# One written order for another: where each part of a fused attention and gated-MLP kernel stands, with the same parts and buffers

## The chip, the core and the metric

The kernel runs on one core of a Trainium2 chip. The metric is the device time of one execution in microseconds (us), lower is better. The engines that matter are TensorE (PE in the profile), VectorE (DVE), ScalarE (ACT), GpSimd (POOL) and SyncE (SP), which issues nearly all loads and stores.

## The reference

Windowed attention (8 batches, 8 heads, 576 positions, head size 64, window 64), its output laid out as 4608 tokens of 512 features, an RMS norm, and a gated MLP (512 to 1536 to 512):

```python
scores = scale * np.matmul(q, k.transpose(0, 1, 3, 2))
scores = np.where((rel >= 0) & (rel < window), scores, -1000000000.0)   # rel = query position - key position
attn = np.exp(scores - np.max(scores, axis=-1, keepdims=True))
attn = attn / (np.sum(attn, axis=-1, keepdims=True) + 1e-09)
x = np.matmul(attn, v)                      # (B, H, S, D), then transposed to (4608, 512)
rms = np.sqrt(np.mean(x * x, axis=-1, keepdims=True) + 1e-06)
xn = x / rms * rms_g
g = xn @ w_gate
silu = g * (1.0 / (1.0 + np.exp(-g)))
return silu * (xn @ w_val) @ w_out
```

## The kernel before

**Tiles.** The 64 heads are 32 pairs, four to a batch. The 4608 tokens are 9 tiles of 512. The 1536 inner features are worked on in chunks. A float32 operand of the MLP is split into a high and a low half-precision part, and a product is then three matmuls (high by high, high by low, low by high), `three` at L1391 to L1393. Tiles 0 and 1 are multiplied so, in groups of 12 matmuls into one PSUM bank. Tiles 2 to 8 use a seven-product scheme (L1694, 12 matmuls each) and outer products (L1633). The weights prepared for these lie in DRAM (`sevens`, `outer`) and are loaded again for every chunk (L1604, L1614), 512 or 768 KB at a time.

**Parts.** The program consists of 3,894 named parts. In the opening (batches 0 and 1 and the first token tiles) the names are a letter and indices: for head pair n, `s` scores on PE, `m` masks on DVE (L735, each followed by an accumulator read), `a` exponential on ACT, `i` sum and reciprocal on DVE (L818, L819), `w` scaling on POOL (L825, L827), `t` transposes on PE (L833), `u` copies, `v` values on PE, `y` take. For the weights: `d` load, `e` exponent on ACT, `p` product on PE (L522), `r` rest on DVE (L526), `t` reduction on DVE (L563, with other indices), `h` and `l` the high and low halves (`l00` and `l01` on DVE, L554). For the normed tokens of tile 0: `F` scaling on DVE (L1299), `H` the high part (L1302, on DVE or ACT by piece), `L` the low part (L1307, on POOL for this tile); `F00x` are a piece of 512 tokens, `F01x` one of 64. `G0cim` is a gate (m = 0) or value (m = 1) group of tile 0, `A M N O P` what follows it. Loads are `q`, `k`, `j`, `d`, `g`. Later parts have numbers: a leading dot is an attention pair (`.10` the scores of a pair, `.10.22` the turn of its mask, DVE L711, after a way through DRAM, L701 and L707; `.11` its values, PE L897; `.65` and `.217` loads of keys and values, `.66` and `.218` the scores that use them), and `+u602` is a product of chunk 6, `+u602.0` the load that follows it into the buffer that it freed; `+o…` are the outer products and `+g…` gate groups of tile 1.

**Order.** `SEQUENCE` (L44 on) writes all parts in one total order. The program emits them in that order, and each engine's queue is then fixed by it:

```python
AT = {n: k for k, n in enumerate(SEQUENCE.split())}
...
for ins in traced[start:]:
    if ins.engine in before and ins.engine in WRITTEN(nc):
        tc.add_manual_dep(ins, before[ins.engine].name, ..., reason="written order")
```

So an instruction waits for the one written ahead of it on its own engine, and for the data and buffers that it needs. `HOMES` gives for each ring of SBUF buffers which buffer the k-th tile takes. A PSUM bank is the one that has been free longest:

```python
def any_bank(name):
    bank_of[name] = free_banks.pop(0)
def done_with(name):
    free_banks.append(bank_of.pop(name))
```

so the order also decides which bank a group gets, and whose last reader it waits for. In this order `G0000`, the first gate group, takes the bank that held half of the scores of pair 5 (`s50`), and the first three masks of `m500` are its last readers. The scores' bank is given back by the mask that reads it last, the bank of the norm's broadcast (`rb`) by the last scaling, `F003`.

Of the kernel before, what the change touches and what calls it, by code (L numbers as in the profile page):

```python
# [52 lines left out]
w411 q7 N000 i50 t411 w501 k6 L010 t410 O000 P000 m511 d30 e301 L013 z11 z12 h10 e300 p210 r210 s60 t20 p211 r211 m600 m601 d40 v40 y40 h11 G0011 t21
z20 p301 d31 u410 u411 p300 t501 y0 l10 a600 a511 z21 A001 z22 l11 z13 a601 z14 w500 t500 u500 M001 v41 G0100 G0110 G0101 y41 N001 x21 h21 a510 e310
e311 r300 i51 s61 r301 t30 u501 A011 M011 v50 i60 h20 m610 m611 l21 w510 t510 u510 p311 r311 O001 w600 P001 p310 a610 A010 w511 G0111 t511 l20 G0200
r310 t31 y50 z30 M010 d41 e411 N011 z31 z32 x30 w601 t601 N010 e410 p410 e400 p411 G0201 r411 r410 q4q a611 i61 w611 w610 t600 z23 u511 u600 e401 O010
v51 y51 k7 s71 u601 q5q P010 z33 j6 .231 s70 m700 a700 v60 m701 p400 r400 a701 h30 l30 m710 A020 i70 m711 t610 .229 G0210 u610 a711 p401 r401 t40 t611
u611 t41 .8 .230 G0211 z40 w701 .0 w700 y60 t700 v61 M020 N020 d50 a710 i71 w711 G0300 d51 e510 e511 p511 A021 t701 x31 M021 N021 w710 p510 h31 z41
z42 h40 A030 j7 r510 e500 G0310 t710 u700 u701 .228 .228.3 l31 y61 x41 r511 d62 u710 O011 O021 P021 t711 G0311 v70 e501 l40 p500 q6q d60 p501 G0301
d63 r500 u711 v71 r501 M030 y70 O020 P020 e621 e620 p621 A031 r621 p620 r620 G0400 b5 d61 e600 P011 M031 N031 .1 e601 h41 t50 t51 O031 e630 z50 p600  # L60
r600 y71 q7q f62 G0410 z43 A041 N030 O030 l41 z51 z52 h50 .230.2 p601 r601 x51 h51 b6 z24 G0401 l50 b7 R1 S1 e631 G0411 p630 r630 p631 r631 B10 F100
A040 F101 F102 F103 .9 P031 M040 N040 f60 O040 B11 l51 H101 H102 G0500 z53 G0511 A050 H103 H100 F110 M041 N041 L100 e610 d65 G0510 e611 A051 p611 L101
F111 p610 .26 L103 G0501 P030 d64 e640 O041 L102 M051 N051 M050 f63 O051 P041 G1000 .234 F112 r611 z34 N050 r610 e641 p640 p641 r640 r641 A100 e650
f61 .2 .2.0 .2.6 .2.5 .2.14 f64 M100 .10 .10.0 .10.5 .10.1 G1011 .10.6 e651 O050 p650 .2.3 .228.1 .228.4 F113 .228.5 .2.7 .233 P051 .10.3 .10.12 H22
p651 .228.6 P040 .2.8 .10.14 r650 r651 f65 G1001 N100 .228.7 .228.8 O100 .17 P100 o0 .228.10 .2.1 G1010 .228.9 .228.11 H11 .228.0 o1 o2 h61 D3 .229.3
.10.7 G1100 G1101 h60 .229.1 .229.4 A110 .2.12 .2.17 .10.8 .10.17 .18 l60 h62 l62 H21 G1110 h64 .10.2 .2.16 .10.4 .10.13 .229.5 .10.11 .2.2 .229.6
.229.7 .229.8 .234.0 .230.0 l61 .2.4 h63 G1111 U10 U30 M110 l64 l63 L11 A111 M111 N111 .229.10 .229.9 .229.11 .10.9 Ht3 A101 Lt3 M101 .236 h65 l65
.231.0 .2.13 .19 N101 .10.10 O101 .19.1 .19.3 .2.10 .235 P101 .19.12 D1 Ht1 U20 .19.0 .19.2 .19.4 .19.11 P050 .2.9 U11 .231.3 U00 Lt1 U21 .2.15 .2.11
# [1940 lines left out]
```

## Time and profile before

| | us |
|---|---|
| median of 3 executions | 934.73 (934.68 to 938.94) |
| the profiled execution | 933.47 |
| its span (first to last instruction) | 931.7 |
| around the span | 1.77 |
| PE busy | 904.0 |
| PE idle | 27.7 |

The span is the stretch that the trace covers; the 1.77 us around it are not in the trace. Times in the rows below are counted from the start of the span. A matmul's length in the trace overlaps that of the next one, so the pace is read from the starts.

### The profile page before, as it was taken

To read this page: it belongs to the slowest core of one execution; us is meant where nothing else is said; L and a number is where in the kernel's file an instruction comes from. 1 tells how busy PE (TensorE), PEld (TensorE's weight loads), DVE (VectorE), ACT (ScalarE), POOL (GpSimd) and SP (SyncE) were. 2 spreads that over 40 slices of the span, in tenths; PEclk is the share of its full clock that TensorE was granted. 3 is DMA by queue.
4 is the path that set the end of the run, shared out by engine and by line. 5 is a ranking of instruction groups with operands and counts; after the bars stand their busy time and mean duration, and the time that the engine had idled before them with its cause. 6 is when DMAs were issued, how large, how long until landed. Compare 5 with 4: busy or idle time off the path is not lost.

```text
span 931.7 us, 22882 instructions
## 1 busy us (share of the span) xinstructions
PE 904.0 (97%) x8581; PEld 688.2 (74%) x8581; DVE 704.1 (76%) x1919; ACT 567.8 (61%) x1473; POOL 413.3 (44%) x486
## 2 busy tenths in 40 slices
PE   5889999999999999999999999999989999999998
PEld 4645554444447885688888888888878888888887
DVE  6899788967797789789767888887777787734760
ACT  5977886744446655667666666776647556524551
POOL 3342562335336353554462666453514645420440
PEclk8889999999999999999999999999999999999999
DMA  8655471368676975787668858975876557546551
GB/s 294 206 177 198 147 256 39 99 184 232 200 225 194 295 279 164 248 299 239 255 203 293 295 177 287 308 245 179 278 268 225 177 163 256 186 138 226 188 159 46
DMA packets 105438, 198.62 MB, mean 213 GB/s; under 512 B 27760, under 2 KB 64624, under 8 KB 105328
## 3 DMA queue, kind: packets, MB, share of 16 engines
q1 hardware_dynamic: 104752, 195.99, 64.9%
q8 instruction: 67, 1.10, 0.5%
q10 hardware_dynamic: 576, 1.18, 0.4%
q14 instruction: 43, 0.35, 0.1%
HBM read 159.39 MB, written 37.75 MB: 212 GB/s over the span
## 4 chain that ended last, share of the span: by engine, by line
PE 74%; DVE 8%; DMA 7%; issue 4%; POOL 3%; ACT 3%; SPq 1%; DVEq 0%; POOLq 0%; ACTq 0%
PE a L1694 31%; PE o L1633 16%; PE po L1391 3%; PE po L1392 3%; PE po L1393 3%; PE sc L722 3%; PE x L897 2%; DMA wt<-sevens 2%; DMA pm<-via 2%; PE pg L1391 2%; PE pg L1392 2%; PE pg L1393 2%; PE pv L1391 2%; PE pv L1392 1%; PE pv L1393 1%
## 5 line engine op out<-in xcount | busy, mean ns | idle before, releaser
L1694 PEld LDWEIGHTS <-wt 128*128 128x128 f16 x3528 | 342.8, 98 | 48.4 <-DMA wt<-sevens 3.4
L1694 PE MATMUL a<-xn,wt 128*128 128x256 f16 x2016 | 237.5, 273 | 1.1 <-DMA wt<-sevens 0.9
L1694 PE MATMUL a<-wt,wt 128*128 128x256 f16 x1224 | 148.1, 273 | 2.0 <-DMA wt<-sevens 1.6
L1731 ACT ACTIVATE th<-a,hsc 128x256 f32<-128x256 f32 x168 | 78.6, 473 | 103.0 <-DVE a L1795 70.1
L1766 POOL TENSOR_TENSOR h<-th,h 128x512 f16<-128x512 f32 x84 | 98.3, 1176 | 81.8 <-ACT h L1764 80.9
L1766 POOL TENSOR_TENSOR wt<-u,wt 128x512 f16<-128x512 f32 (+1 forms) x72 | 67.5, 939 | 134.8 <-ACT wt L1764 88.2
L1633 PE MATMUL o<-wt,h 128*128 128x256 f16 x864 | 100.3, 273 | 0.2 <-DVE o L1655 0.2
L1795 DVE TENSOR_TENSOR a<-a,s 128x512 f32<-128x512 f32 x90 | 62.1, 693 | 48.8 <-PE a L1694 43.8
L1633 PEld LDWEIGHTS <-h 128*128 128x128 f16 x864 | 84.0, 98 | 11.4 <-issue 1.4
L1726 DVE SCALAR_TENSOR_TENSOR th<-th,a 128x256 f32<-128x256 f32 x168 | 69.2, 412 | 29.0 <-ACT th L1731 27.6
L738 ACT ACTIVATE pm<-pm,st 128x128 f32<-128x128 f32 (+1 forms) x216 | 83.8, 390 | 11.0 <-DVE st L735 10.8
L693 POOL TENSOR_TENSOR pm<-pm,st 128x512 f32<-128x512 f32 (+1 forms) x72 | 60.2, 864 | 46.7 <-DVE st L767 25.6
L1727 DVE SCALAR_TENSOR_TENSOR th<-a,th 128x256 f32<-128x256 f32 x168 | 71.3, 424 | 5.8
L1633 PEld LDWEIGHTS <-wt 128*128 128x128 f16 x648 | 63.3, 98 | 8.5 <-issue 1.2
L1712 ACT COPY s<-a 128x512 f32<-128x512 f32 x90 | 52.2, 582 | 22.0 <-PE a L1694 19.2
L1764 ACT CAST h<-th 128x512 f16<-128x512 f32 x84 | 51.2, 615 | 13.5 <-DVE th L1742 7.9
L735 DVE CUSTOM_DVE_ANT_0 pm<-sc,blocked 128x128 f32<-128x128 f32 x192 | 48.9, 281 | 12.5 <-PE sc L722 12.3
L1391 PE MATMUL po<-wt,h 128*128 128x512 f16 x136 | 51.6, 379 | 0.0
L1392 PE MATMUL po<-wt,h 128*128 128x512 f16 x136 | 51.5, 379 | 0.0
L1393 PE MATMUL po<-wt,h 128*128 128x512 f16 x136 | 51.5, 379 | 0.0
L722 PE MATMUL sc<-kv,q 64*64 64x128 f32 (+1 forms) x1056 | 43.5, 291 | 5.9 <-DMA q<-q 4.9
L1633 PE MATMUL o<-wt,wt 128*128 128x256 f16 x432 | 49.1, 273 | 0.0
(235 smaller groups left out, 1757.0 us busy)
## 6 DMA issues: line engine op xcount, KB each, us to landing
wt<-sevens SPq DMA_DIRECT2D x84, 512.0 KB, 5.1
wt<-sevens SPq DMA_DIRECT2D x42, 768.0 KB, 5.7
wt<-outer SPq DMA_DIRECT2D x24, 768.0 KB, 5.7
kv<-kv SPq DMA_DIRECT2D x28, 608.0 KB, 5.7
via<-pm SPq DMA_DIRECT2D x96, 144.0 KB, 2.7
pm<-via SPq DMA_DIRECT2D x24, 576.0 KB, 4.7
q<-q SPq DMA_DIRECT2D x28, 288.0 KB, 4.7
st<-w_gate SPq DMA_DIRECT2D x6, 1024.0 KB, 6.8
```

Source lines behind the costliest of these rows:

```text
L722: nc.tensor.matmul(out.rearrange("p (n c) -> p n c", c=D), lhsT=qt[hd, j * D : (j + 1) * D], rhs=halves[hd, :1, :] if j == 0 else halves[h ...
L738: nc.scalar.activation(part, part, AF.Exp, bias=low, scale=-1.0, accum_out=total)
L1391: nc.tensor.matmul(acc, lhsT=lh, rhs=rh, start=first, stop=False)
L1392: nc.tensor.matmul(acc, lhsT=lh, rhs=rl, start=False, stop=False)
L1393: nc.tensor.matmul(acc, lhsT=ll, rhs=rh, start=False, stop=last)
L1633: nc.tensor.matmul(acc[:, sub * HT : (sub + 1) * HT], lhsT=l[:, x, sub * P : (sub + 1) * P], rhs=r[:, y, :], start=first and c == cs[0] an ...
L1694: nc.tensor.matmul(acc[:, i * HT : (i + 1) * HT], lhsT=ws[l][:, kt, :], rhs=b[:, m, kt, :], start=at_start, stop=kt == 1 and j == 2, skip_ ...
L1726: nc.vector.scalar_tensor_tensor(cols, cols, 1.0, acc[:, :HT], ALU.add, ALU.mult)
L1727: nc.vector.scalar_tensor_tensor(cols, acc[:, HT:], 2.0**-42, cols, ALU.mult, ALU.mult)
L1731: nc.scalar.activation(cols, acc[:, :HT], AF.Tanh, scale=th_scale[:, c : c + 1])
L1766: nc.gpsimd.tensor_tensor(lo, src, hi, ALU.subtract)
L1795: nc.vector.tensor_tensor(to, acc, kept.pop((c, name)), ALU.add)
```

## The change

One part of the file is replaced: the text of `SEQUENCE`, and with it `HOMES`. The same 3,894 names stand in another order; no part, no shape, no engine of an instruction and no number of buffers is changed. With the order change which buffer of its ring a tile takes (`HOMES` is the list for the new order), which PSUM bank a group takes, and when each load is issued. The diff, cut to the stretches that the prediction speaks of:

```diff
@@ -42,190 +42,190 @@
 SEQUENCE = """
-q0 k0 s00 q1 q2 m000 a000 m001 a001 i00 k1 s10 s01 m010 j1 c10 m100 w001 a010 a100 k2 s21 m011 a011 j0 g0 m101 a101 g1 j2 s11 w000 t000 t001 c21 g2
...
-b3a y31 q3q b3 R0a e200 S0a R0 S0 z01 z02 z03 B00a B00 F001 F002 H002 F000 F003 L002 e100 e101 p100 s41 p101 a400 d11 e110 r101 B01 F010 r100 e201 k5
-p201 j5 q5 s50 H003 F012 H001 e111 p110 a401 F011 i40 L001 r110 H000 L000 w400 m410 h01 s51 m411 d21 H010 F013 h00 l00 p111 m500 a500 m501 p200 r111
-w401 a411 t401 L003 G0000 l01 H012 L012 r200 t400 t10 a501 t11 r201 e210 A000 z10 a410 i41 G0001 H011 L011 u400 u401 H013 w410 M000 e211 m510 G0010
...
-.10.22 .37 +g1200.0 +g1200.1 +g1201 +g1201.0 .11 +g1201.0.0 .12 +g1310 +g1310.0 .234.2 .19.21 .238 .13 .19.22 .20 .21 .234.1 .234.4 .234.5 E0 .234.6
...
-+u602 +u605.0 .189.15 .188.21 +u606 .188.22 +u602.0 +u602.1 .189.16 .189.17 +u602.2 +o542 +u606.0 .189.18 .200.18 .189.19 .200.19 +u602.2.0 .189.20
-+u603 +o542.0 +o542.1 +o542.2 .192.22 +o542.2.0 .189.21 +u611 +u603.0 +u612 +u603.1 +u603.2 +u603.2.0 +u607 +u611.0 +u616 +u607.0 +u604 +u604.0
-+u612.1 +u612.2 +u612.2.0 .209 .209.0 +u607.1 +u607.1.0 +u604.1 .209.2 .209.11 .209.5 .216 .200.20 .193 .194 .209.6 +u615 .195 .196 +u615.0 +u607.2
-+u607.4 +u604.1.0 .209.1 +u607.5 +u621 +u621.0 +u622 +u607.3 .209.7 +u616.0 +u607.6 .209.8 +u612.0 +u613 .209.3 +u613.1 +u613.2 .209.4 .209.10 .227
-.209.16 +u607.7 +u604.2 +u604.4 +u613.2.0 +u617 +u617.0 +u617.1 .217 +u622.1 +u626 +u626.0 +u617.1.0 +u617.2 +u607.8 +u632 +u625 +u625.0 +u631 +u614
-+u622.2 .200.21 +u617.4 .200.22 +u622.2.0 +u613.0 +u631.0 +u632.1 .218 .218.2 .218.1 .209.15 +u614.1 .218.7 .209.14 .218.0 .218.5 .209.9 +u622.0
...
+q0 k0 s01 m010 q2 j0 c01 s00 m000 m001 k1 q1 s10 m011 a010 m100 a000 a001 i00 a011 i01 g0 g1 g2 a100 m101 c00 a101 i10 d00 e001 e000 w000 t000 u000 k2
...
+q3a b3a y31 z01 z02 R0a q3q b3 S0a R0 S0 e110 e111 p110 p111 e101 B00a r111 B00 q5 F000 d20 h00 k5 s50 F002 F001 e200 H000 L000 r110 H002 L002 e201
+p201 p200 q7 e100 p101 p100 l00 q6 a411 H001 L001 F003 m500 r201 a500 H003 L003 z03 r100 h01 B01 G0000 r101 l01 G0001 a401 a400 k6 r200 i40 w400 t400
+t10 t11 m501 d21 e210 e211 a410 p210 z10 u400 j5 i41 r210 p211 F010 F011 A000 M000 r211 j4 d30 G0011 z11 a501 w411 e300 w401 F012 w410 F013 t401 z12
...
+.233.7 .233.8 .233.10 +g1401 +g1201.0 .28.10 .28.12 .10.22 .233.9 .233.11 +g1201.0.0 +g1210.0 +g1210.1 .36 +g1211.0 .28.9 .28.16 .28.18 .28.19 .28.20
+.235.1 +g1300 +g1300.0 +g1500 +g1500.0 +g1300.1 +g1301.0 +g1301.0.0 +g1201.0.1 .251 +g1501 .19.22 .234.1 +g1500.1 +g1501.0 .11 .13 .20 .12 .234.3
...
+.209.11 .192.19 +u602.1 +u602.2 +u606 .200.16 +o572.0 +u606.0 +o542 +o542.0 .189.8 +u611 +u602.2.0 .209.7 .189.21 .189.5 .209.10 +o572.2.0 +u611.0
+.189.22 .216 .192.20 .209.13 .189.6 +u603 +o542.2 +u603.1 .200.9 .200.14 .200.15 .200.12 .200.18 +u616 +u603.2 +u603.2.0 +u602.0 +u607 +u607.0 .192.21
+.189.10 +u612 +u612.1 +u607.1 +u607.1.0 +u615 +u607.2 +u607.4 .209.0 +u615.0 .209.8 +u612.2 +u607.5 +u604 +u613 +o542.1 +u621 .192.22 .193 .209.9
++u607.3 +u604.1 +u616.0 +u607.6 +u613.1 +u613.2 .200.19 .200.20 .194 .209.15 .195 +u613.2.0 +u604.1.0 .189.14 .196 +u607.7 +u604.2 +u621.0 +u617
++u617.0 +u604.4 +u604.6 .209.17 +u622 +u622.1 .209.12 +u625 +u625.0 +u614 +u617.1 .209.16 +u603.0 +u626 +u626.0 +o542.2.0 +u612.2.0 +u617.1.0 +u617.2
++u617.4 +u604.0 +u622.2 .217 .218 .218.1 .218.6 .218.5 .197 .218.7 +u614.1 +u604.3 .209.18 .209.19 +u612.0 +u622.0 .189.18 +u623 +u607.8 .218.3
++u617.5 +u617.7 +u623.1 +u623.2 +u614.0 +u622.2.0 .218.12 +u627 +u623.2.0 +u627.0 +u627.1 +u617.3 .218.15 +u627.1.0 +u604.5 +u631 +u631.0 .218.10
++u613.0 +u635 +u624 +u624.1 .200.21 +u632 .218.14 +u614.1.0 +u617.6 .200.22 .218.0 +u635.0 +u627.2 .218.16 +u627.3 +u623.0 +u614.3 .189.19 .218.8
...
```

In words: `F003` stands later among DVE's parts and is now what frees `G0000`'s bank; `G0000` and `G0001` come ahead of other parts of the opening; `.11` stands two groups further behind `.10.22`; the loads `+o542.0`, `+u602.0` and `+u612.0` change places.

## Rows read from the trace of the kernel before

**Rows 1.** Page, part 1: busy us (share of the span) and instructions of each engine.
```profile
PE 904.0 (97%) x8581; PEld 688.2 (74%) x8581; DVE 704.1 (76%) x1919; ACT 567.8 (61%) x1473; POOL 413.3 (44%) x486
```

**Rows 2.** Windows of the span: length, busy us (x instructions) by engine, PEclk, DMA share, GB/s.
```profile
6.37:54.68 48.31, 37.08 (x425) 26.14 (x426) 41.30 (x197) 38.60 (x120) 20.36 (x32) 0.82 0.70 243
54.68:58.90 4.22, 4.22 (x12) 1.65 (x13) 4.19 (x11) 3.60 (x15) 0.84 (x1) 0.60 0.52 165
58.90:97.00 38.10, 37.43 (x321) 20.38 (x319) 33.87 (x101) 28.41 (x68) 15.56 (x25) 1.00 0.57 193
```

**Rows 3.** Waits of PE, 0 to 195 us: total us, times, longest us.
```profile
PE pg L1391 <- DVE st L735: 2.2, 2, 2.0
```

**Rows 4.** Waits of PE, 195 us to the end.
```profile
PE a L1694 <- DMA wt<-sevens: 2.5, 3, 1.6
PE x L897 <- DVE pm L711: 1.7, 2, 1.2
PE s L722 <- ACT pm L738: 1.1, 1, 1.1
PE a L1694 <- DVE xb L979: 0.4, 1, 0.4
```

**Rows 5.** Timeline of PE around the first gate group: start, length, instruction, [idle before <-releaser].
```profile
50.84 0.66 PE L722 MATMUL sc<-kv,q 64*64 64x128 f32 x14 [0.93 <-DVE wt L526]
...
52.30 0.38 PE L833 MATMUL tr<-ident,p 128*128 128x128 f32 x2
54.68 0.38 PE L1391 MATMUL pg<-xn,wt 128*128 128x512 f16 x1 [2.00 <-DVE st L735]
...
55.70 0.63 PE L1392 MATMUL pg<-xn,wt 128*128 128x512 f16 x1
...
58.68 0.44 PE L1393 MATMUL pg<-xn,wt 128*128 128x512 f16 x1
...
59.28 0.38 PE L1391 MATMUL pv<-xn,wt 128*128 128x512 f16 x1
...
61.88 0.38 PE L1391 MATMUL pg<-xn,wt 128*128 128x512 f16 x1
```

**Rows 6.** Timeline of DVE, same stretch.
```profile
51.94 2.03 DVE L554 SCALAR_TENSOR_TENSOR wt<-wt,ws 128x1024 f16<-128x1024 f32 x1
53.90 0.28 DVE L735 CUSTOM_DVE_ANT_0 p<-sc,blocked 128x128 f32<-128x128 f32 x1
...
55.86 1.28 DVE L554 SCALAR_TENSOR_TENSOR wt<-wt,ws 128x1024 f16<-128x1024 f32 x1
```

**Rows 7.** Timeline of POOL, same stretch.
```profile
51.74 1.16 POOL L1307 TENSOR_TENSOR xn<-xb,xn 128x512 f16<-128x512 f32 x1
```

**Rows 8.** DVE by line and form, 43 to 54.6 us: busy us, mean ns | idle before.
```profile
L526 DVE SCALAR_TENSOR_TENSOR wt<-st,pw 128x512 int32<-128x512 int32 x3 | 2.0, 674 | 0.0
...
L1299 DVE SCALAR_TENSOR_TENSOR xb<-xb,gsb_late,rb 128x64 f32<-128x64 f32 x4 | 1.0, 272 | 0.0
L1302 DVE CAST xn<-xb 128x512 f16<-128x512 f32 x2 | 0.8, 422 | 0.0
L818 DVE TENSOR_SCALAR st<-st 128x5 f32<-128x5 f32 x1 | 0.7, 735 | 0.0
```

**Rows 9.** Window 55.5 to 58.8 us, columns as in the windows above.
```profile
55.50:58.80 3.30, 3.30 (x9) 1.18 (x8) 3.30 (x5) 2.78 (x10) 0.84 (x1) 0.50 0.45 123
```

**Rows 10.** Timeline of PE at two later gaps.
```profile
227.34 0.88 PE L897 MATMUL x<-pm,kv 64*64 64x128 f32 x23 [1.22 <-DVE pm L711]
...
679.75 1.48 PE L1694 MATMUL a<-wt,wt 128*128 128x256 f16 x12 [1.62 <-DMA wt<-sevens]
```

**Rows 11.** Page, part 6: size of one load, median us to landing.
```profile
wt<-sevens SPq DMA_DIRECT2D x84, 512.0 KB, 5.1
...
kv<-kv SPq DMA_DIRECT2D x28, 608.0 KB, 5.7
```

**Rows 12.** One line, 660 to 720 us: the loads from sevens.
```profile
DMA to landing us min/median/max: 3.8/7.2/9.0
```

More of the change, by code (lines that the diff above doesn't have):

```diff
@@ L53 @@
[L53 to L68, printed above, removed]
@@ new lines @@
+q3a b3a y31 z01 z02 R0a q3q b3 S0a R0 S0 e110 e111 p110 p111 e101 B00a r111 B00 q5 F000 d20 h00 k5 s50 F002 F001 e200 H000 L000 r110 H002 L002 e201
+p201 p200 q7 e100 p101 p100 l00 q6 a411 H001 L001 F003 m500 r201 a500 H003 L003 z03 r100 h01 B01 G0000 r101 l01 G0001 a401 a400 k6 r200 i40 w400 t400
+t10 t11 m501 d21 e210 e211 a410 p210 z10 u400 j5 i41 r210 p211 F010 F011 A000 M000 r211 j4 d30 G0011 z11 a501 w411 e300 w401 F012 w410 F013 t401 z12
+u401 i50 w500 s51 m510 m511 h10 v40 a510 t411 t410 t20 G0010 e301 p300 d31 H011 A001 H010 L011 L010 u410 u411 e310 l10 d40 p301 H012 r301 L012 G0100
@@ new lines @@
+a511 H013 L013 t500 M001 N001 d41 t21 u500 v41 s60 O001 j7 P001 e311 i51 w510 p310 y40 y41 p311 e401 h11 G0110 z20 r300 w501 j6 z13 A011 m600 m601 z21
+l11 y0 t501 u501 z22 z23 z14 e400 G0111 r310 N000 .8 x21 h21 h20 l20 p401 r401 p400 t510 G0101 r400 A010 M010 a601 a600 i60 d60 u510 w600 w601 s61
+M011 N011 e411 m610 v50 G0200 O011 N010 O000 e410 t600 t30 r311 t31 z30 l21 m611 G0210 A021 A020 O010 z31 z32 x31 h31 P011 w511 P000 p410 r410 x30
+t511 k7 h30 a610 d50 M021 d51 d61 t601 P010 .230 u600 y50 G0201 t40 M020 N020 a611 i61 p411 G0211 e500 N021 O021 r411 l30 G0300 w611 t41 z40 u511 v51
@@ new lines @@
++u231.0 .48.22 .66.14 +u224 +u227.1 +u233 +u227.1.0 +u236 +u224.1 +u214.1.0 +u214.2 +u236.0 .49 .51 +u222.0 +u245 +u232.1 +u232.2 .240.1 +u245.0
++u233.1 +u233.2 .66.15 z34 +u232.2.0 .240.2 +u214.0 +u224.1.0 y1 .57.20 +u233.2.0 +u232.0 +u241 .50 +u237 +u237.0 .240.3 +u237.1 +u237.1.0 +u214.3
++u233.0 .52 +u255 +u234 .45 +u234.1 .57.21 +u227.2 .84 +u234.1.0 .37.22 .57.22 +u223.0 +u241.0 +u242 .53 +u243 .66.17 +u242.1 +u242.2 +u224.0
++u242.2.0 +u237.2 .54 .66.18 +u234.2 +u234.0 .66.19 +u237.3 +u246 +u243.0 +u246.0 .77 .58 .60 .59 +u224.2 +u243.1 +u234.3 .66.20 .66.21 .61 +u251
@@ new lines @@
+.75.5 .75.11 .75.16 +u302 .75.12 .75.15 .241.9 .242.8 .74.9 .94 .95 .95.2 .86.12 .95.7 .86.13 .95.6 .95.5 .95.8 .74.22 .243.2 .95.0 +k232 +k233
++k205.0 +u301 +k225.0.0 +u301.0 .242.9 +u244.0 +u302.1 .78.20 .78.21 .75.17 .75.13 +u305 .243.3 .74.19 +u305.0 +u306 .86.10 +u306.0 .243.4 .95.1
+.74.10 +u303 +u302.2 +u303.1 +u303.2 +k214 .75.14 .86.18 +k205.0.0 .75.6 .95.14 .243.5 +u307 +u302.0 .95.3 .243.6 .95.12 +k215 .243.8 +u303.2.0
++u307.0 +u304 .75.20 +u311 +u315 .75.18 +u307.1 .95.4 +u303.0 +u304.1 +u307.1.0 +u307.2 +k215.0 .75.9 .86.19 +k215.0.0 .86.20 .75.21 .75.19 .95.11
@@ new lines @@
++o572.1 .209 .188.21 .200.13 +o532.1.0 .209.2 .188.14 .200.11 .209.5 .188.19 .189.12 .189.13 .209.14 .200.10 +o572.2 .189.15 .189.20 .209.1 +u605
++u605.0 +u554.5 .188.6 +o522 .189.17 .189.9 .209.6 +o522.0 +o522.1 .192.8 .192.17 .188.22 .209.3 .209.4 +o540 +o541 .192.18 +u601 +u601.0 +u602
+.209.11 .192.19 +u602.1 +u602.2 +u606 .200.16 +o572.0 +u606.0 +o542 +o542.0 .189.8 +u611 +u602.2.0 .209.7 .189.21 .189.5 .209.10 +o572.2.0 +u611.0
+.189.22 .216 .192.20 .209.13 .189.6 +u603 +o542.2 +u603.1 .200.9 .200.14 .200.15 .200.12 .200.18 +u616 +u603.2 +u603.2.0 +u602.0 +u607 +u607.0 .192.21
@@ L224 @@
++o860 +o852.0 +o852.1 +o861 +o862 +o830 +o862.0 +o862.1 +o862.2 +o831 +o832 +o870 +o832.0 +o832.1 +o871 +o832.1.0 +o872 +o822 +o872.0 +o872.1 +o872.2
++o840 +o822.0 +o872.2.0 +o822.1 +o841 +o822.1.0 +o842 +o842.0 +o842.1 +o842.2 +o842.2.0
 """
```

302 lines of the change are left out of this document (149 added, 153 removed).

## The prediction

> **What bounds the kernel now.** First the page's part 1: PE is busy for 904.0 of 931.7 us [rows 1], so no order can give more than the 27.7 us in which PE idles, plus what its clock loses. The windows come next, to see where that lies. From 6.37 to 54.68 us PE works 37.08 of 48.31 us at a granted clock of 0.82, while DVE works 41.30 [rows 2]: the opening is DVE's, and PE waits for it. From 54.68 to 58.90 PE is full, but at a mean clock of 0.60 [rows 2]. After 97 us only single waits are left. The waits of PE name them. In the opening the gate groups wait 2.2 us for masks of DVE, nearly all in one wait of 2.0 [rows 3]. After 195 us it is 2.5 us for weights from `sevens` (three waits, the longest 1.6), 1.7 for a mask turned on DVE (two, the longest 1.2), 1.1 at scores and 0.4 on an output of DVE [rows 4]. The timelines show the two places that matter most. `G0000` starts at 54.68, after 2.00 us without work; its matmuls then start 0.43 us apart from 55.70 on, and its last one starts at 58.68, so PE goes on at 58.9; the next group takes 2.60 (59.28 to 61.88) [rows 5]. 0.43 against 0.217 is the half clock, 1.2 against 2.4 GHz, and the window of 55.5 to 58.8 shows 0.50 [rows 9]. On DVE, what runs in front of those masks is `l00`, 2.03 us [rows 6].
>
> **The opening.** The instructions are the same, so the change costs or gives only waits and clock. `G0000` waits for the last reader of its bank. Before, that is the third mask of `m500`; in the new order it is `F003`. I count DVE's parts ahead of either, by the prices of DVE's forms [rows 8]. Ahead of it in the old order alone stand `r101` and `r100` (0.60 each, the pitch of a 0.674), `F010` to `F013` (0.19 each, the pitch of a 0.272, so 0.76), `i40` (0.74 and a short reciprocal, 0.85), `H003` and a small high part (0.34 and 0.21) and three masks (0.21 each, 0.63): 3.99. In the new order alone stands `r111`: 0.60. DVE reaches the release 3.4 us sooner, at about 51.3 in place of 54.7. That holds if DVE idles as much as before (7.0 us in 48.3 [rows 2]).
>
> Nine of the 12 matmuls can then go. The last three need the low part `L003` on POOL, which needs `H003` on DVE, and in the new order `m500` (0.8) and `r201` (0.6) are queued on DVE ahead of `H003`. So `H003` is done at 51.3 + 0.8 + 0.6 + 0.42 = 53.1 [rows 8] and `L003`, 1.16 us [rows 7], at 54.3. The group ends at 54.9 if the clock is full and at 55.6 if its last three run at 0.43; if all 12 run at 0.43 it ends at 51.3 + 5.2 = 56.5. Before, it ended at 58.9 [rows 5]. That is a gain of 2.4 to 4.0; I take 3.3, since the row is that of a PE that had idled, and this one idles again before the last three. Work that was done before `G0000` must come off: the second half of the scores of pair 5 (`s51`, 0.43 and 0.66 with an overlap, 1.02 [rows 5]) and the transposes `t401` (two, 0.22 [rows 5]) now follow it, 1.24 in all. **The opening: −2.1, between −1.2 and −2.8.** It costs nothing elsewhere as long as the groups behind `G0000` find their operands ready. The narrowest of these is `G0111`: counted by the same prices, DVE's parts through `l11`, which it needs, add up to 62.9 us against 59.0, while the PE work ahead of it falls from 50.0 to 46.1. Its slack was near 8 us by that count and is near none. I cost it at nothing; the rival below costs it.
>
> The first loads change places too: `j0` goes ahead of `k2`, `d00` ahead of `k2`. The value copy `c01` is early on DVE and needs `j0`, so a late `j0` would hold the masks behind it. The count of bytes puts `k2` some 3 us later, just in front of its scores. I cost this at 0, with 0.5 either way.
>
> **Locks between DVE and POOL.** `l00` took 2.03 us and `l01`, the same form, 1.28 [rows 6]; `l00` started at 51.94, while POOL's `L003` ran from 51.74 to 52.90 [rows 7]. The 0.75 between them is the overlap's price here. The Trainium skill (SBUF — State Buffer, "SBUF: two separate sides") says that a DVE operation with two SBUF inputs and a GpSimd operation that reads SBUF hold the shared port pair by turns, each for its whole instruction; the trace agrees, as `l00` ends 1.07 us after `L003`. It speaks against this change at one place: `l00` and `L002` are both released by `H002` in the new order, so one may wait for the other there, and a wait of up to a whole `L` part, 1.16, would be an estimate from the row. In the sum `l00` keeps its 2.03, so that neither the 0.75 nor a second one is counted.
>
> **Later waits.** (1) `.11`: between the turn and the values stands one gate group on PE, 2.6 us; in the new order three, 7.8. The wait of 1.22 [rows 10] goes: −1.2. (2) `+u616` waited 1.62 [rows 10]; what it lacks is the load `+o542.0`, which was issued behind `+u602.0` and others. In the new order it is issued ahead of `+u602.0`. Landing took 9.0 us at the longest in this stretch [rows 12] against a median of 5.1 [rows 11], while the PE work from its release to `+u616` stays 7.8 us. With 5.1 to about 8 for landing 0 to 0.4 of the wait stays: −1.2. Sooner issue alone is no gain if the bytes then share the same engines; the Trainium skill (DMA: Bandwidth & Descriptors, "Issuing engines are not separate DMA queues") says that all queues run on the same 16 engines and interleave. The 9.0 against 5.1 agrees, and the wait would keep its 1.6 if it held here in full. (3) The other two waits for `sevens`, 2.5 − 1.6 = 0.9 [rows 4]: the load `+u612.0` had 5 products between release and use, about 6.5 us, and now has some 15: −0.9. (4) The 0.4 on DVE's output [rows 4]: its lead grows to 6 us, −0.4. (5) The 1.1 at scores and the second turned mask (0.5) keep their order: 0. New risks: `.218` follows its keys' load `.217` by 6.5 us of PE work instead of 11.8, against a median landing of 5.7 [rows 11], and some leads over DVE fall below 1 us: +0.8 together, between 0 and 2. **Later: −2.9, between −4 and −1.**
>
> **Sum.** −2.1 − 2.9 = −5.0. The profiled execution took 933.47, 1.26 less than the median; taken from its span the changed kernel's would be 926.7 (928.5 with the 1.77 around it), and the median 934.73 − 5.0 = 929.7.
>
> **Rivals.**
> *More than that.* If PE, working closer together, keeps 2.4 GHz through `G0000` and the groups before it, or if DVE idles less than 7.0, the opening gives more: half of DVE's idle time, 3.5, and 1.7 of clock (half of the 3.3 us at 0.50 [rows 9]) on top: about 924.5. For it: PE ran at a mean of 0.82 there [rows 2], which is 8 us lost. Against it: PE still waits for the same DVE, and only a few parts stand closer.
>
> *The opening gives nothing, the later loads only part.* If `l00` and `L002` lock each other (up to 1.16), `c01` holds the masks and `L003` comes last, the 2.1 is gone; if `+o542.0` shares the engines and lands as late as before, 1.2 of the later gain is gone too. What is left is −1.7: 933. This is also the case that the change doesn't do what it says.
>
> *Slower.* `G0001` to `G0111` stand closer, so that PE gets to weights that DVE has not split yet. DVE was busy for 33.87 of 38.10 us from 58.9 to 97 [rows 2], so it can't catch up fast. Each such stop would be as the one before `G0000`: 2.0 of gap [rows 5] and 1.7 of half clock behind it, 3.7. One or two of them eat the gain; from three on (11 us) it is slower: 934.7 − 5.0 + 11 = 940.7. For it: the slack at `G0111` is near none. Against it: by the count only that group is near none, and the masks and scalings that were put ahead of `l11` are short.
>
> **How the numbers follow.** I give my forecast 0.48, more than that 0.12, the opening eaten 0.25, slower 0.15. The predicted time is that of the likeliest, 929.7; its own range is 927.5 (all terms at their better end, −7) to 932.5 (−2.2). About 0.5%, 4.7 us, is what a measurement of this kernel can tell from no change: 930.1 and 939.4 are the bounds. The first bound lies only 0.4 above the middle of my forecast, so of its 0.48 I count 0.30 as faster; with the 0.12 of the second case and 0.03 of the third that makes 0.45. Slower by 0.5% needs three stops or more: 0.12. The rest, 0.43, is the same. The range from 922 to 937 leaves out the cases of three stops and a clock that gains more than 12 us.
>
> **What would show it.** Right: `G0000` starts near 51 us with a gap inside it before its last three matmuls; no wait at `.11`; the waits for `sevens` fall from 2.5 to under 0.7; the window before 97 us ends some 2 us sooner for the same matmuls. Wrong: a clock well above 0.82 in the opening (more), `l00` over 2 us beside an `L` part on POOL with `G0000` no sooner (eaten), or gaps on PE released by `wt` of DVE, with 0.50 behind them, between `G0001` and `G0111` (slower). The forecast falls if DVE, and not the release of one bank, sets the time of `G0100` to `G0111`: then nothing of the 2.1 arrives.

## The result and the profile after

The changed kernel takes 919.9 us (median of 4, 919.24 to 921.96) against 935.37 for the kernel before beside it: a ratio of 0.9831, interval 0.9801 to 0.9861, so 13 to 18.6 us faster. The forecast was 929.7 with a range of 922 to 937; the gain is three times the 5.0 us that were forecast, and the time lies below the range. The page's head and its part 1:

```profile
span 917.5 us, 22880 instructions
...
PE 895.5 (98%) x8581; PEld 685.9 (75%) x8581; DVE 696.3 (76%) x1919; ACT 568.2 (62%) x1473; POOL 417.3 (45%) x486
```

The span is 14.2 us shorter than before (931.7). PE's busy time fell by 8.5 us and its idle time from 27.7 to 22.0. The windows, with the columns of [rows 2]:

```profile
6.37:54.68 48.31, 40.20 (x445) 26.39 (x441) 44.75 (x212) 45.67 (x139) 22.61 (x33) 0.96 0.82 288
54.68:58.90 4.22, 4.22 (x54) 2.96 (x53) 4.12 (x19) 2.90 (x8) 1.63 (x4) 1.00 0.59 166
58.90:97.00 38.10, 37.69 (x305) 20.45 (x304) 35.40 (x94) 29.24 (x66) 20.07 (x26) 1.00 0.49 163
```

From 6.37 to 54.68 us PE now works 40.20 us in place of 37.08 and DVE 44.75 in place of 41.30, at a granted clock of 0.96 in place of 0.82; the half clock of 54.7 to 58.9 is gone. In the last row PE's and the clock's figures are nearly those of [rows 2]. So most of the gain lies ahead of 60 us. I also counted it by work, taking each part of PE at a short time that these traces show for it, and asking when that much was done. By this rough count the changed kernel is some 10 us ahead where before stands at 65 us and still 10.3 at 218; then 13.8 at the end. The forecast had 2.1 up to 218 us and 2.9 behind it.

The clock over the three stretches in which before ran at half (14.7 to 24.3, 41.9 to 48.3 and 55.7 to 58.6 us). First two of them in before, for the third see [rows 9]; then all three in the changed kernel, and the one such stretch that is left there:

```profile
14.70:24.30 9.60, 7.41 (x70) 5.83 (x71) 7.95 (x44) 7.27 (x27) 2.65 (x6) 0.50 0.58 202
41.90:48.30 6.40, 6.28 (x41) 3.72 (x44) 5.43 (x16) 6.40 (x16) 3.06 (x5) 0.50 0.48 140
```

```profile
14.70:24.30 9.60, 7.73 (x123) 5.58 (x124) 9.28 (x50) 8.44 (x32) 3.21 (x7) 1.00 0.95 338
41.90:48.30 6.40, 5.71 (x21) 2.62 (x21) 6.35 (x18) 6.23 (x19) 5.49 (x5) 0.73 0.70 218
55.70:58.60 2.90, 2.90 (x46) 2.16 (x47) 2.80 (x17) 2.57 (x7) 0.87 (x2) 1.00 0.58 140
42.60:45.40 2.80, 2.80 (x7) 1.13 (x7) 2.80 (x10) 2.63 (x7) 2.36 (x3) 0.50 0.49 118
```

19 us at 1.2 GHz became 3. PE's timeline and DVE's around `G0000`, answering to [rows 5] and [rows 6]:

```profile
42.59 0.58 PE L522 MATMUL pw<-mn,unit 128*128 128x512 bf16 x1 [1.41 <-ACT mn L516]
...
45.85 0.38 PE L1391 MATMUL pg<-xn,wt 128*128 128x512 f16 x1
...
48.24 0.38 PE L1393 MATMUL pg<-xn,wt 128*128 128x512 f16 x1
48.45 0.38 PE L1391 MATMUL pv<-xn,wt 128*128 128x512 f16 x1
```

```profile
42.93 1.28 DVE L554 SCALAR_TENSOR_TENSOR wt<-wt,ws 128x1024 f16<-128x1024 f32 x1
44.12 0.74 DVE L1299 SCALAR_TENSOR_TENSOR xb<-xb,gsb_late,rb 128x512 f32<-128x512 f32 x1
...
46.31 0.42 DVE L1302 CAST xn<-xb 128x512 f16<-128x512 f32 x1
```

`G0000` starts at 45.85, not at 54.68 and not at the forecast 51.3; in this trace it takes 2.6 us up to `G0001` (48.45), at full clock, without a stop (a second trace has two stops, below). `F003` (44.12) is done at 44.87, and `l00` (42.93) takes 1.28. On POOL, the two low parts that start at 43.09 take 3.25, where one takes 1.16:

```profile
43.09 3.25 POOL L1307 TENSOR_TENSOR xn<-xb,xn 128x512 f16<-128x512 f32 x2 [0.44 <-DVE xn L1302]
46.81 1.16 POOL L1307 TENSOR_TENSOR xn<-xb,xn 128x512 f16<-128x512 f32 x1 [0.46 <-DVE xn L1302]
```

The waits of PE after 195 us, answering to [rows 4]:

```profile
PE a L1694 <- DVE a L1795: 1.5, 3, 0.6
PE a L1694 <- DMA wt<-sevens: 0.9, 1, 0.9
PE x L897 <- DVE th L1438: 0.7, 1, 0.7
PE x L897 <- DVE pm L711: 0.4, 1, 0.4
```

The waits at `.11`, `+u616`, `+u632` and `+u345` are gone. New ones stand at `+u507` (0.9, for `sevens`) and inside the values of the pair behind `.11` (0.7, `L1438`). All waits of PE after 195 us are some 4 us against 5.9.

### The profile page after: what moved, and what is told of

Read it like the earlier page. It is cut to its first block, busy times and chain, and to the rows that moved or that the text cites. A ratio compares the mean times of both kernels' runs of the same rounds, so it can differ in the third digit from the quotient of the medians.

```text
span 917.5 us, 22880 instructions
## 1 busy us (share of the span) xinstructions
PE 895.5 (98%) x8581; PEld 685.9 (75%) x8581; DVE 696.3 (76%) x1919; ACT 568.2 (62%) x1473; POOL 417.3 (45%) x486
## 4 chain that ended last, share of the span: by engine, by line
PE 80%; DVE 9%; DMA 4%; ACT 2%; issue 2%; SPq 1%; POOL 1%; ACTq 0%; DVEq 0%; POOLq 0%
PE a L1694 36%; PE o L1633 17%; PE sc L722 3%; PE po L1391 3%; PE po L1393 3%; PE po L1392 3%; PE x L897 3%; PE pv L1391 2%; PE pv L1393 2%; PE pv L1392 1%; PE pg L1391 1%; DMA out<-ot 1%; PE pg L1393 1%; PE pg L1392 1%; DMA via<-pm 1%
## 5 line engine op out<-in xcount | busy, mean ns | idle before, releaser
L1766 POOL TENSOR_TENSOR h<-th,h 128x512 f16<-128x512 f32 x84 | 98.4, 1182 | 67.7 <-ACT h L1764 61.5
L1766 POOL TENSOR_TENSOR wt<-u,wt 128x512 f16<-128x512 f32 (+1 forms) x72 | 66.8, 932 | 130.1 <-ACT wt L1764 75.9
L1795 DVE TENSOR_TENSOR a<-a,s 128x512 f32<-128x512 f32 x90 | 62.5, 695 | 48.3 <-PE a L1694 35.2
L1712 ACT COPY s<-a 128x512 f32<-128x512 f32 x90 | 52.2, 584 | 27.7 <-PE a L1694 25.7
L1764 ACT CAST h<-th 128x512 f16<-128x512 f32 x84 | 51.3, 616 | 11.6 <-DVE th L1742 5.9
L735 DVE CUSTOM_DVE_ANT_0 pm<-sc,blocked 128x128 f32<-128x128 f32 x192 | 48.5, 283 | 8.2 <-PE sc L722 8.2
L1633 PE MATMUL o<-wt,wt 128*128 128x256 f16 x432 | 49.8, 273 | 0.0
L722 PE MATMUL sc<-kv,q 64*64 64x128 f32 (+1 forms) x1056 | 41.6, 284 | 7.3 <-DMA q<-q 5.7
```

The lines of the kernel that those rows point to most:

```text
L722: nc.tensor.matmul(out.rearrange("p (n c) -> p n c", c=D), lhsT=qt[hd, j * D : (j + 1) * D], rhs=halves[hd, :1, :] if j == 0 else halves[h ...
L1633: nc.tensor.matmul(acc[:, sub * HT : (sub + 1) * HT], lhsT=l[:, x, sub * P : (sub + 1) * P], rhs=r[:, y, :], start=first and c == cs[0] an ...
L1766: nc.gpsimd.tensor_tensor(lo, src, hi, ALU.subtract)
L1795: nc.vector.tensor_tensor(to, acc, kept.pop((c, name)), ALU.add)
```

## The experiments

Two theories were held against each other. **C (clock):** PE's closer work keeps 2.4 GHz, and 16 us less at half clock are the gain. **D (DVE):** DVE's queue sets the opening; the order changes what stands in it ahead of `G0000`, what it waits for and how long it takes, and PE's clock only follows. "Ahead" below is the start of `G0500` (134.1 us before) where a kernel keeps the old order there; a second trace of before has it at 134.5, one of the changed kernel 0.9 later than the first (124.4 for 123.5), so differences below 1 us are not read, and each such figure is that of one trace. Changes of the time come from the ratio to before beside it, times 935.

### Which stretch: the two orders joined

An order can be joined from two: the first parts as one kernel has them, all other parts in the other's order.

```diff
 x36:  the first 165 parts of the new order (up to u311), then the rest in the old one
 x48:  the first 255 of the new order (up to j4), then the old one
 x225: the first 945 of the new order, then the old one
 y225: the first 945 of the old order, then the new one
```

> The first 165 parts stand in the new order (the opening attention, up to u311, where PE stood at 36 us before and at 32 us after), all the rest in the old one. Theory C (clock): the first long stretch at half clock, 14.7 to 24.3 us before, goes with the 2.5 us stop ahead of it, and 3 to 4 us of the 15 come from here. Rival D (DVE's queue ahead of the first gate group sets the opening): DVE's idle time up to 36 us shrinks by 2.5 to 3, so -2 to -3, and the clock adds nothing of its own. Rival M (the later waits carry most of it): below 1 us.

Measured: ratio 0.9966 (0.9943 to 0.9989), so -3.2 us (-5.3 to -1.0); 4.3 ahead at `G0500` (129.8), as `G0000` is (50.4). This lies in the ranges of both theories and doesn't part them.

> The first 255 parts in the new order (up to j4, some parts behind G0001), the rest in the old one. Theory C: the second and third stretch at half clock (41.9 to 48.3 and 55.7 to 58.6 us) go as well, G0000 starts near 46 instead of 54.7, and -9 to -11 stand. Rival D: G0000 starts as early, but what follows waits for DVE, which has the same work left; -5 to -7. Rival M: -2.

Measured: 0.9960 (0.9937 to 0.9983), -3.7; `G0000` starts at 45.6, but at `G0500` (128.6) only 5.5 are left, which is theory D's 5 to 7; at the end it is less. Where the old order takes over, the transposes wait 1.8 us for POOL's scaling. What was gained at `G0000` holds only with the order behind it; the 9 to 11 of theory C were missed.

> The first 945 parts in the new order (up to about 218 us, the wait at .11 left in the old stretch's hands), the rest in the old one. The division by the two traces: -11 to -13. Rival M: -5 or less, with the rest in the later loads.

Measured: 0.9886 (0.9856 to 0.9915), -10.7 us (-13.5 to -7.9).

> The other half: the first 945 parts in the old order, the rest in the new one. The forecast's later terms: -2.9. The division by the two traces: -2 to -3. Rival M: -8 or more.

Measured: 0.9970 (0.9952 to 0.9987), -2.8 us (-4.5 to -1.2). The two halves add up to 13.5 of the 15.8. The opening is where the forecast was short. Of the later terms `y225` doesn't hold the first: `.11` is the 899th part of the old order and the 910th of the new, so it is among the first 945 and keeps its old place here. The forecast for the rest was -1.7, and the interval holds it.

### The clock by itself

Extra matmuls in an unused part of a bank fill PE's stops in the kernel before; nothing reads them and nothing else is changed.

```diff
             box["gpb"] = any_bank("gpb")
+            for _ in range(10):
+                nc.tensor.matmul(box["gpb"][:, P : 2 * P], lhsT=ident, rhs=ident, start=True, stop=True)
```

> The kernel before, with 10 extra matmuls of 128x128 into an unused part of the bank of g4, in the 2.5 us in which PE stands still from 12.33 us on; their results are read by nobody, nothing is left out and no order is changed. Theory C (clock): PE stays at 2.4 GHz through 14.7 to 24.3 us, the work of that stretch is done 2.5 to 3.5 us sooner, and 2 to 3 of it last to the end. Rival D (DVE sets the opening): DVE has the same queue, so below 1 us, whatever the clock does.

Measured: 1.0019 (1.0001 to 1.0037), so slower if anything; 0.8 ahead at `G0500`. The windows of 14.7 to 20.9 and of 20.9 to 24.8 us:

```profile
14.70:20.90 6.20, 3.50 (x52) 2.59 (x51) 5.80 (x36) 5.86 (x26) 1.67 (x4) 1.00 0.90 319
20.90:24.80 3.90, 3.86 (x31) 1.97 (x32) 3.78 (x13) 3.48 (x9) 1.20 (x3) 0.57 0.16 48
```

The clock did stay at 1.00 up to 20.9, where before it was 0.50 from 14.7. PE then only waited longer: 2.4 us for `c01` on DVE in place of 2.1. From 20.9 on the half clock is back (0.57), so 6.2 of the first stretch's 9.6 us were tried.

> As f_g4, with extra matmuls also ahead of R0a (4), behind z01 (4) and behind t401 (8), in the stops of 0.96, 0.95 and 2.0 us. Theory C: the three stretches at half clock go (19.3 us), PE's busy time falls by 7 to 9 us apart from the extra work, and -5 to -7 at the end. Rival D: the granted clock rises, PE waits longer for DVE instead, and the time stays within 2 us.

Measured: 0.9993 (0.9978 to 1.0008). One window, and DVE's `l00` and `m500` in it (lines are numbered 2 to 6 higher in this kernel):

```profile
27.00:50.00 23.00, 19.29 (x246) 14.03 (x238) 19.73 (x81) 20.92 (x55) 10.34 (x15) 1.00 0.59 190
```

```profile
51.96 2.03 DVE L556 SCALAR_TENSOR_TENSOR wt<-wt,ws 128x1024 f16<-128x1024 f32 x1
53.91 0.28 DVE L741 CUSTOM_DVE_ANT_0 p<-sc,blocked 128x128 f32<-128x128 f32 x1
```

From 27 to 50 us the clock is 1.00, through the whole of before's second half-clock stretch, and DVE's `l00` starts at 51.96 and `m500` at 53.91: 51.94 and 53.90 in [rows 6]. Not one tenth of a microsecond came of it. For this stretch and, by `f_g4`, for most of the first one theory C falls. (`G0000` starts at 57.2, since the eight matmuls behind `t401` ran at half clock and went on past the release.)

### DVE's order

```diff
 m_c01:  ... u000 u001 e000 s20
+c00 c01
 m200 c11 a200 t010 u010 i21
-c00 c01
 v00 ...
```

> The kernel before, with c00 and c01 (copies of values on DVE) moved ahead of m200, into a stop of DVE of 1.29 us; the second half of v00 waited 2.06 us for c01. Theory C: the wait goes, but the half clock stays, -1.5 to -2. Rival: the wait moves to the next part of the chain (u010) and it is 0.

Measured: 1.6 ahead at `G0500` (132.5); the time 0.9994 (0.9975 to 1.0012), so nothing of it shows at the end.

```diff
 m_l00:  ... H010 F013 h00
-l00
 p111 m500
+l00
 a500 m501 ...
```

> The kernel before, with l00 moved behind m500, so that it no longer runs beside L003 on POOL. If the port is what it seems: l00 takes 1.28 in place of 2.03, G0000 starts some 0.7 us sooner and the time falls by 0.7, and by up to 1.7 more if the shorter stop keeps the clock. Rival: the time of 2.03 is not of the port, l00 takes 2.0 again, and the time is the same or 0.5 longer.

Measured: `l00` takes 1.28, and `G0000` starts at 52.9, 1.8 sooner, since all of `l00` and not only its 0.75 left the way of the masks; inside the group PE then waits 0.9 for `l00`. 1.1 ahead at `G0500` (133.0); the time 0.9997 (0.9975 to 1.0018), not to be told from before.

```diff
 m_queue: F010 F012 F011 F013 H010 i40 w400 moved from ahead of m500 to behind m501; w401 a411 t401 behind G0000
```

> The kernel before, with F010 to F013, H010, i40 and w400 moved behind m501 and w401, a411 and t401 behind G0000: 1.8 us less of DVE's work ahead of the masks that free G0000's bank, all else in the old order. Theory D: G0000 starts 1.5 to 2 us sooner, -1.5 to -2 at 100 us, and 0 to -2 at the end. Rival (the bank's release is not what G0000 waits for): it starts at 54.7 as before.

Measured: the release does come sooner, `G0000` starts at 52.5; but the group then stops for 2.7 us, and 1.1 us are lost at `G0500` (135.2); the time 1.0018 (0.9997 to 1.0040). PE's waits from 40 to 62 us:

```profile
PE pg L1392 <- POOL xn L1307: 2.7, 1, 2.7
PE pg L1391 <- DVE st L735: 1.5, 1, 1.5
```

`w400` now waits for the later `i40` and stands ahead of `L003` on POOL, so `L003` starts at 56.25. My edit moved the wait to another queue; as a test of the release it holds, as a repair it fails.

```diff
 m_open: c00 c01 ahead of m200; l00 behind m500; F010 F012 F011 H010 F013 behind m501
```

> Three edits of DVE's order in the kernel before, all else as it was: c00 and c01 ahead of m200, l00 behind m500, F010 to F013 and H010 behind m501. Theory D: they add up, 1.9 + 1.2 + 1.0, about -4 at 100 us, whatever the clock is; at the end -2 to -4, as far as the later waits leave it. Rival: PE's clock or another engine takes it back, and less than 2 us are left at 100 us.

Measured: 2.0 ahead at `G0500` (132.1), half of what was expected; the time 0.9985 (0.9960 to 1.0011), which can't be told from no change either. The three don't add up: with `F013` later, its bank comes back later, by the rule of the free banks `G0000` takes the next one, and that is the other half of pair 5's scores, whose last reader is `m501`. `m500` is done at 51.3, `G0000` starts at 53.3, right behind `m501` (53.17).

```diff
 m_d00: ... k1 ... a010 a100
+d00
 k2 s21 ... g4
-d00
 w011 ...
```

> The kernel before, with one load issued sooner and nothing else moved: d00 (1 MB of w_gate) ahead of k2 in place of behind g4. Theory D: sooner issue alone shares the same engines, which show 1.05 (full) from 5 to 18 us; e000 stays behind the same parts on ACT at 17.7 us, k2 lands up to 2.7 us later, and the time is the same or up to 1 us longer at 40 us. Rival (the loads set the opening): e000, e001 and r001 come sooner, -1 to -2 at 40 us.

Measured: 1.0006 (0.9980 to 1.0032), and 1.6 us behind at `G0500` (135.7). The exponent of the load that was issued sooner, `e000`, in this kernel and in before:

```profile
19.03 1.21 ACT L516 ACTIVATE mp<-st,consts 128x1024 bf16<-128x1024 int8 x1
```

```profile
17.68 1.21 ACT L516 ACTIVATE mp<-st,consts 128x1024 bf16<-128x1024 int8 x1
```

Issued 3.9 us sooner (2.11 for 6.03), the megabyte landed 2.3 us sooner and is used 1.35 us later: behind it `k2` landed at 11.6 us in place of 8.4 and `j0` at 12.5 in place of 9.3, and the parts ahead of `e000` wait for these.

```diff
 y36: the first 165 parts of the old order, then the rest in the new one
```

> The first 165 parts in the old order, the rest in the new one: what the first 36 us are worth inside the changed kernel. Theory D (DVE's queue sets the opening, PE's clock follows): the 4.3 us that x36 showed at 36 us are missing, the later gains stay: -15.5 + 4.3, about -11. Rival S (starting sooner helps only in part, since later loads and waits take it back, as in x36, whose 4.3 us at 200 us were 2.7 at the end): -13 to -15.

Measured: 0.9894 (0.9867 to 0.9920), -9.9 us (-12.4 to -7.5), against -15.8 with the new opening: the first 36 us are worth some 6 inside the changed kernel, as theory D had it (about -11), and more than the 3.2 that they are worth alone. At `G0500` (131.5) they are worth 7 to 8.

```diff
 a_l00 (the changed kernel):  H002 L002 ...
-l00
 q6 a411 H001 L001 F003 m500 r201 a500 H003
+l00
 L003 ...
```

> The changed kernel, with l00 moved from behind H002 to behind H003, so that it runs beside L003 on POOL again and ends last ahead of G0000's second matmul. Port theory: l00 takes about 2.0 in place of 1.28, G0000 comes 1.5 to 2 us later, PE may fall to half clock behind it, and +1.5 to +3 at 100 us. Rival: POOL waits instead of DVE (L002 shows 2.1 in the changed kernel), the group comes at most 1 us later, and 0 to +1.

Measured: PE waits 1.2 us for `l00` inside `G0000`, and `G0001` starts at 49.8, where two traces of the changed kernel have 48.5 and 49.4; at `G0500` (124.6, against 123.5 and 124.4) nothing is left that can be read, and the time, 0.9866 (0.9833 to 0.9898) of before, can't be told from 0.9831. `l00` itself took 1.27 and not 2.0: the port theory was wrong about who pays. DVE and POOL:

```profile
45.19 1.23 DVE L1302 CAST xn<-xb 128x512 f16<-128x512 f32 x1
46.34 1.27 DVE L554 SCALAR_TENSOR_TENSOR wt<-wt,ws 128x1024 f16<-128x1024 f32 x1
```

```profile
44.98 1.16 POOL L1307 TENSOR_TENSOR xn<-xb,xn 128x512 f16<-128x512 f32 x1 [0.76 <-ACT xn L1302]
46.50 2.13 POOL L1307 TENSOR_TENSOR xn<-xb,xn 128x512 f16<-128x512 f32 x1 [0.36 <-DVE xn L1302]
```

`l00` starts 0.16 ahead of `L003` and takes 1.27; `L003` takes 2.13. In [rows 6, 7] `l00` started 0.20 behind, and it was `l00` that took 2.03. In both, whichever starts second pays. The cast `H003` (45.19) took 1.23 beside `L001` (44.98) on POOL, where it takes 0.42 alone.

### The later loads

```diff
 m_o542:  ... .188.22
-+u602.0
 +u602.1 ... +u603 +o542.0
-+o542.1
 +o542.2 ... +u611 +u603.0
++u602.0 +o542.1
 +u612 ...
```

> The kernel before, with the loads +u602.0 and +o542.1 moved behind +u603.0, so that +o542.0 is issued alone and 2 to 3 us ahead of them. The forecast's step: +o542.0 lands in 5 to 6 us, the wait of 1.62 at +u616 goes, -1.2 to -1.6. Rival: the load lands as late, or the next waits (0.9 at +u632 and +u651) grow by what was saved: 0 to -0.4.

Measured: the time is 0.9975 (0.9955 to 0.9995), -2.3 us (-4.2 to -0.5). The wait at `+u616` is shorter and not gone:

```profile
682.24 1.48 PE L1694 MATMUL a<-wt,wt 128*128 128x256 f16 x12 [0.87 <-DMA wt<-sevens]
```

`+o542.0` was issued at 674.22, 4.2 us ahead of the next load from `sevens`, and still took 8.0 us to land, as the rival said; a load of keys and values went out 0.5 us ahead of it. Nor can the 0.87 be put down to the edit: three kernels that keep the old order of these loads show 0.56, 0.66 and 0.82 there (`m_queue`, `m_open`, `x225`), two traces of before 1.62 and 2.04. Other waits stand in this trace (1.4 for keys and values at scores, 1.2 on DVE). Where the 2.3 come from stays open.

> The kernel before once more, unchanged, for a second trace. If the later waits belong to the order, the waits of PE after 195 us are the same to 0.3 us (2.5 on sevens, 1.7, 1.1). If they move with the execution, their places or sizes differ by a us or more, while the starts of the gate groups up to 195 us are the same to 0.3 us.

> The changed kernel once more, unchanged: the same question. Theory D: G0000 at 45.9 and G0500 at 123.5 within 0.3 us; the waits after 195 us stay below those of before in sum.

Measured: 935.32 and 920.13 us. The opening is the same to some 1 us (`G0000` at 54.8 and 45.9, `G0500` at 134.5 and 124.4, the last 0.9 later than in the first trace, where 0.3 was expected). The later waits of before moved:

```profile
PE a L1694 <- DMA wt<-sevens: 2.6, 2, 2.0
PE s L722 <- ACT pm L738: 1.2, 1, 1.2
PE s L722 <- DMA kv<-kv: 0.6, 1, 0.6
...
PE x L897 <- DVE pm L711: 0.4, 1, 0.4
```

In before 2.6 for the weights in two waits, the turned mask 0.4 in place of 1.7, two new ones; in sum 6.3 (5.9 in the first trace). In the changed kernel the sum is 3.8 (4.0); its one wait for `sevens` is 1.4, at `+u507` again. So the sum of the later waits belongs to the order, and the size of a single one partly to the execution.

## Why the prediction was right or wrong

**The later waits: the size right, in part by luck.** Forecast -2.9 (-4 to -1); `y225` measured -2.8 (-4.5 to -1.2), but holds only terms worth -1.7, so the size is met within a wide interval and not more. Term by term:

- `+u616`, `+u632` and `+u345` no longer wait in any of the five traces with the new later order (`after`, `after2`, `a_l00`, `y36`, `y225`). The load for `+u616` lands there 4.0 to 4.3 us after its issue, sooner than the 5.1 to 8 of the forecast. That its place ahead of `+u602.0` does this is not shown: in `m_o542` it had that place and took 8.0.
- The 1.2 at `.11` belonged to one execution. In the thirteen traces with the old order there the wait lies between 0 and 1.22, in before's second trace at 0.38. In the five with the new order it is gone, and PE waits 0.3 to 1.0 us inside the next pair's values instead.
- The waits for `sevens` were to fall under 0.7. They are 0.9 and 1.4 in the two traces of the changed kernel, at `+u507`, which the forecast didn't have. The 1.1 at scores, priced at 0, is gone.

The trace kept of `y225` doesn't show its -2.8 in waits: PE waits 5.4 us after 195 us, 2.7 of it at 253 us, where neither kernel waits.

**The opening: the term that failed.** -2.1 was forecast, some 10 to 11 came. The mechanism was right in kind: `F003` frees the bank, and in `after2`, `x48` and `x225` `G0000` starts within 0.1 us of its end. The step that failed is the count of when DVE gets there: it took DVE's idle time as unchanged, priced the order of the first 36 us at 0, and kept stretched instructions at their old prices. DVE's work and idle time up to the release, in before (two windows) and in the changed kernel:

```profile
0.00:36.50 36.50, 25.36 (x331) 18.83 (x333) 25.69 (x146) 25.98 (x93) 14.41 (x35) 0.86 0.73 257
36.50:54.53 18.03, 13.08 (x122) 8.49 (x117) 16.12 (x60) 13.76 (x26) 8.46 (x11) 0.81 0.67 217
```

```profile
0.00:36.50 36.50, 25.86 (x380) 19.64 (x380) 28.15 (x167) 28.98 (x100) 15.89 (x36) 1.00 0.79 286
0.00:44.87 44.87, 32.07 (x424) 23.33 (x425) 35.92 (x190) 37.32 (x111) 18.83 (x38) 0.97 0.76 271
```

Before, DVE reached the release at 54.53 us with 41.80 of work and 12.7 of idle time; now at 44.87 with 35.92 and 8.95. The release comes 9.7 us sooner (8.7 in the second trace of the changed kernel: 45.80, with the same work and 9.9 idle):

- 3.4 of it were in the forecast: the parts that no longer stand ahead.
- 3.8 are idle time (2.8 in the second trace). "That holds if DVE idles as much as before" was the step, and it didn't hold. DVE's waits up to the release, before and then in the changed kernel:

```profile
DVE p L735 <- PE sc L722: 6.9, 4, 4.5
DVE st L818 <- ACT p L738: 1.7, 3, 0.9
...
DVE xb L1299 <- PE rb L1271: 0.7, 1, 0.7
...
DVE rm L1205 <- PE tot L1070: 0.5, 1, 0.5
```

```profile
DVE p L735 <- PE sc L722: 5.4, 4, 4.2
...
DVE st L818 <- ACT p L738: 0.3, 1, 0.3
```

The masks wait 1.5 us less for scores and the sums 1.4 less for exponentials. Both lie in the first 36 us, whose order I had costed "at 0, with 0.5 either way" by looking at loads alone. The other 1.2 are waits for PE in the norm. In the first 36.5 us DVE works 28.15 us in place of 25.69, and `x36`, which has only that part of the new order, shows nearly the same:

```profile
0.00:36.50 36.50, 26.61 (x383) 20.05 (x383) 27.87 (x162) 27.95 (x99) 15.90 (x36) 1.00 0.85 294
```

- 2.5 are work that got shorter (41.80 - 35.92 = 5.9, less the 3.4): instructions that were held up. `l00` is 0.75 of it. The prediction had the two numbers side by side and left them out of the sum. Three small operations for the norm's weights (L453, L489, L490) took 1.55 us together before and 0.57 now. The rest are the sums of the opening (L818) and smaller ones.

Behind the release, `G0000` was forecast to stop before its last three matmuls for `L003`. In the first trace it doesn't: PE had other products to do until 45.85, and `L003` came at 47.97, in time. In the second it stops twice, the second time for `L003`:

```profile
47.33 0.38 PE L1392 MATMUL pg<-xn,wt 128*128 128x512 f16 x1 [0.43 <-POOL xn L1307]
...
48.96 0.38 PE L1392 MATMUL pg<-xn,wt 128*128 128x512 f16 x1 [0.17 <-POOL xn L1307]
```

`x48` and `x225` show the same two stops. So the group takes 2.6 us in one trace and 3.5 in three, where before took 4.2 at a half clock, and that adds most of the rest. `s51` and `t401` stand behind `G0000` now; what they cost there (1.24 in the forecast) was not measured.

**The rival "more than that"** named both sizes, DVE's idle time (3.5; it was 3.8 and 2.8) and the clock (1.7), and got 0.12. The first was right. The second is the better story and false as a cause: PE's busy time did fall by 8.5 us, but `f_g4` and `f_all` gave most of the first two stretches' clock back without the order, and less than 1 us came of it by `G0500`, and none at the end. For the third, `G0000`'s own, `m_o542` helps by chance: its opening is that of before, and its `G0000` ran at full clock all the same. It was 0.9 us ahead at `G0011` (66.8 for 67.7), and at `G0100` nothing was left (72.7 in both), since PE waited for DVE in between:

```profile
71.24 0.35 PE L571 MATMUL n<-sq,one 128*128 128x2 f32 x2 [0.59 <-DVE sq L567]
```

Where PE waits for DVE, a faster PE waits longer. A low clock does cost where DVE waits for PE. In the second trace of the changed kernel the half clock fell on other work, PE's broadcasts for the norm; the ten of them took 2.18 us, and DVE waited for them:

```profile
37.30:40.70 3.40, 3.21 (x13) 2.55 (x12) 2.24 (x12) 3.37 (x4) 0.00 (x0) 0.50 0.93 366
```

```profile
40.95 2.07 DVE L1299 SCALAR_TENSOR_TENSOR xb<-xb,gsb_late,rb 128x512 f32<-128x512 f32 x3 [1.09 <-PE rb L1271]
```

In the first trace these scalings start at 40.01, without a wait. The 0.9 us are found again at the release (45.80 for 44.87) and at `G0500` (124.4 for 123.5).

**The rival "the opening gives nothing"** had its lock: `L002` and the part behind it took 3.25 on POOL. In the first trace it cost nothing, since PE got there late; in the second, in `x48` and in `x225` it is the stop of 0.43 above. The Trainium skill (SBUF — State Buffer, "SBUF: two separate sides") says that whichever of the two starts first has the pair for its whole instruction; the traces agree at both signs (2.03 for DVE, second by 0.20 us; 2.13 for POOL, second by 0.16).

**The rival "slower"** didn't come: `l11` ends at 69.14 in the changed kernel, `G0111` starts at 69.06, and no wait shows there. The slack was near none, as counted, and it was enough.

**Not settled:** which moves of the first 36 us shorten DVE's waits. `m_c01` alone is 1.6 at `G0500`; a load moved alone is a loss; the rest was not taken apart. The split of the 9.7 us is read from the traces, not built up by experiments: the edits of DVE's order in the kernel before gave 2.0 at most of the 10 at `G0500`, and none of them a change of the time that its interval tells from none.

## What to carry to other kernels

- In a stretch that one engine's queue sets, count three things up to the first big consumer: what stands ahead, how long the engine idles, and which of its instructions are stretched. Another order changes all three; the trace of the old order gives only the first.
- A low clock of the engine that waits is a symptom. Before it is priced, fill its stops with work that nobody reads: if the queue that it waits for doesn't move, the clock is worth nothing there. It costs where that queue waits for the slow engine, as the second trace of the changed kernel shows.
- Take a second trace of the same kernel before a single wait is priced. The wait at `.11` was 1.22 us in one and 0.38 in the next, and a group without a stop had two.
- Moves are not additive: a part moved on one engine changed which bank came free next (`m_open`), and what stood in front on another queue (`m_queue`). A big load issued sooner without its users is a loss while the DMA engines are full (`m_d00`).

## What the runs showed of the hardware that was not expected

Stops of PE didn't set the clock by their length. In the changed kernel a stop of 1.79 us and one of 1.55 were followed by 1.00, and the one of 1.41 at 42.59 by 0.50 from 42.6 to 45.4:

```profile
11.03 0.37 PE L474 MATMUL gps<-ident,gmx 128*1 128x128 f32 x1 [1.79 <-DVE gmx L470]
```

```profile
22.49 0.71 PE L722 MATMUL sc<-kv,q 64*64 64x128 f32 x18 [1.55 <-DVE pt L842]
```

In the second trace of the same kernel the stop at the same place (43.53, for `mn`) was longer, 1.60 us, and 42.6 to 45.4 shows 1.00; there the half clock had come from 37.3 to 40.7. What PE did around the stops differs, and no run here takes that apart.
